# A single-core packed-attention and gated-convolution kernel: another issue order for the same instructions

## The chip, the cores and the metric

The kernel runs on one core of a Trainium2 chip. The metric is the device time of one execution in microseconds. Its engines, as the profile names them, are TensorE (PE, with PEld for the loads of its stationary operand), VectorE (DVE), ScalarE (ACT), GpSimd (POOL) and SyncE (SP), which issues all of the kernel's transfers (SPq). PSUM is the memory into which PE writes.

## The reference

Two attentions in a row, then a gated convolution with two matrix products. Batch 8, 8 heads, 576 positions, head size 64, 32 packed queries; the model width is 512.

```python
def sm_attn(qq, kk, vv):
    s = scale * np.matmul(qq, kk.transpose(0, 1, 3, 2))
    s = s - np.max(s, axis=-1, keepdims=True)
    a = np.exp(s)
    a = a / (np.sum(a, axis=-1, keepdims=True) + 1e-09)
    return np.matmul(a, vv)
p_packed = sm_attn(p, k, v)
out = sm_attn(q, p_packed, p_packed)
...
for k in range(K):
    gate_pre += conv_w[k][None, None, :] * xp[:, k:k + S, :]
gate = 1.0 / (1.0 + np.exp(-gate_pre))
val = x @ w_val
return (gate * val @ w_out).astype(np.float32)
```

`x` is the attention's output with the heads side by side, and `xp` is `x` with four rows of zeros ahead. The three weights come as double-precision numbers.

## The kernel before

Each of the eight batches goes through the same steps, and every kind of step is a Python generator (in the list `streams`) that issues a few instructions and then yields. Which generator goes on next is set by a long string, `ORDER`: a token such as `v0` takes the generator `v` of batch 0 one yield further, `v0.3` three yields, and a bar ends the stage in which the double-precision weights are turned into pairs of single-precision ones. The class `InOrder` makes each engine issue its instructions in exactly the order in which the tokens made them, SP's transfers too. So the string is the order, on all engines at once, and an instruction that waits holds up everything behind it on its engine.

The letters of the tokens, with the names that the instructions have in the profile:

- `K`, `V`, `Q`, `P`, `L`: transfers issued by SP. K and Q of a batch come in two halves (km, qm), V in two halves (vm) and a small rest (v), P for two batches at a time (p), the weights as blocks (cw_words, wv_words, wo_words).
- `C`: the convolution's weights; PE writes cwps. `W`: the value weights. `O`: the output weights, split into woh and wol by ACT, DVE and POOL.
- `k`, `q`: K and Q turned. In batches 0 and 1 PE turns them (kt, qt, and pTt for P), ACT copies them out; from batch 2 on DVE does it (kT, qT).
- `a`: the first attention, on the packed queries: scores s1 on PE, the row's maximum nb on DVE, the exponential on ACT, transposes at on PE, copies a1t on ACT, the product with V (pv) on PE.
- `p`: the packed result turned (ppTt on PE). `c`: the taps of the convolution multiplied in (ppk on POOL). `w`: the packed result times the value weights (wp on PE, wph and wpl).
- `s`, `t`: the second attention: scores s2 on PE, transposes t, maxima mx and sums sm on DVE, the subtraction and the scaling on POOL (DVE in batch 0), the exponential on ACT, and from them a, a2h and a2l.
- `g`: the gate, in two halves (gate on PE, sig on ACT). `v`: the value product, in two halves of two blocks (val on PE, then sig on DVE, gvh on ACT, gvl on DVE).
- `o`: the last product with woh and wol. Two batches together have nine chunks of 128 rows; o_2_1 is chunk 1 of batch 2's list. A chunk is 12 products on PE, a copy osb on ACT and two stores by SP. An even batch makes the chunks 0 to 3 of its pair, an odd one 4 to 8. The last batch makes its five chunks side by side, and only the last quarter of each chunk by itself.

In this text an index behind a name is the batch, and behind it the half or block: gate_2_1 is the second half of batch 2, val_0_1_0 the first block of the second half of batch 0.

What binds the order is the memory in which PE writes: one buffer `quad` for s1, s2 and gate, one buffer `big` for cwps, pv, wp and val, and two buffers `mid` for the transposes and the chunks of o. Each must have been read by ACT or DVE before the next one writes to it. Of K and Q there are five buffers together (`m`), of V two, of osb two, and of the weight blocks five.

The tokens run in two parts, before and behind the bar:

```python
before, after = ORDER.split("|")
with tc.tile_pool(name="stage", bufs=1) as stage:
    run(before)
late = ctx.enter_context(tc.tile_pool(name="late", bufs=1))
gvh = late.tile([P, NC, 2 * S], F32R, name="gvh")
gvl = late.tile([P, NC, 2 * S], F32R, name="gvl")
run(after)
```

gvh and gvl lie where the stage had its memory, so they wait for the last step on the weights. All instructions are recorded in the helper `InOrder`, so every row of the profile has its line, L61; the names tell the steps apart.

Of the kernel before, what the change touches and what calls it, by code (L numbers as in the profile page):

```python
# [26 lines left out]


ORDER = """
K0 P0 k0.6 K0 L0 C0.2 L0 k0 Q0 L0 Q0 k0.2 C0.4 k0.3 V0 k0.2 k1 k0 W0.2 a0 C0 V0 L0 q0.5 k1 a0.3 q0 k1 C0 q0 a0 q0 a0  # L30
q0.2 a0.4 C0 W0.5 V0 W0 a0.2 W0.6 L0 q0.2 W0 a0 L0 a0 p0 W0.2 p0.2 C0 W0.2 p0 O0.2 s0 W0.2 C0 W0 O0 K1 k1 K1 V1 W0
O0 s0 k1 s0 k1.2 Q1 k1.2 s0.2 k1.2 W0.2 s0 W0 O0.2 k1 O0 w0 k1 s0 Q1 t0 L0 V1 k1 c0 O0 w0 k1 s0 q1 s0 t0 a1 t0 q1.2
t0 q1 a1.3 V1 q1 t0 O0 q1 a1 c0 O0 q1.2 P2 t0.2 W0.2 w0 t0.2 a1.5 q1 O0.2 L0 O0 L0 K2.2 a1.2 t0 a1 O0 a1 O0 t0.2 q1
k2 O0 p1 O0 p1 k2 O0 g0 O0.3 p1 g0 O0.6 K3 q1 O0 k2 p1 q1 O0.3 k2 g0.2 O0.5 v0 O0.2 c1 v0 V2 O0 s1.2 O0 | v0 s1 v0.3
s1.2 a2 v0 s1 a2 v0 s1.2 V2 v0 k3 v0 V3 t1.2 v0 a2 s1 a2 o0 V2 v0 t1 o0 v0 a2 o0 v0 a2.2 t1.2 a2 t1 a2 v0 w1.2 t1 a2
o0 k3 t1 o0 a2.2 w1 Q2.2 K3 t1 c1 t1 a2 t1.2 g1 a2 v1 p2 k3.2 K4 P4 V4 p2 g1 p2 q2 k4 v1 p2 a3 o0 v0 Q3 K4 a3 V4
a3.3 q2 a3 v1.2 o0 v1 k4 a3 o0 s2.2 o0.2 s2.2 v1 s2 k4 a3 o0 s2 Q3 s2 v1.2 s2 a3 k5 k4 g1 v1 g1 t2 o0 t2 V3 a3 V3
a3.2 v1 a4 t2.2 s2 a4 t2 a4 c2 a4.2 k5 a3 o1 a3 K5 v1 q3 K5 o1.3 t2 o1.2 v1 t2 a4 t2.2 v1 t2 p3 v1 P6 a4 t2 a4.2 c2
a4 t2 p3 w2 V5 v1 w2 v1 g2 V4 w2 p3 Q4 o1 q3 g2 V5 k5.2 p3 Q5 a4.2 Q4 s3 o1 a4 s3.6 g2 a4 k6 s3 t3 v2 g2 v2 o1.2 s3
v2 p4 t3.2 Q5 t3 v2.2 K7 t3 v2 p4 o1 p4 o1 t3 v2 t3.2 a5.2 v2.2 o2 v2.2 a5 o2 q4 V6 v2.2 V6 p4 a5.3 o1 v2 o1 c3 a5  # L40
q4 t3.2 s4 c3 t3 s4.3 a5.2 s4 w3 t3 g3 o1 w3.2 a5 s4 g3 v3 s4 o2 t4 k6 v3 K6 v3.2 a5 t4.3 g3 v3.2 g3 q5 v3 c4 o2
v2.2 K6 v3.2 k6 a5 o2 q5 v3 Q6 k6 o3.3 V5 o2 v3.4 s4 a6.2 a5 a6 s4 K7 V7 a5 a6 V7 c4 t4.2 p5.2 o2 p5 a6 k7 a6 p5 o2
t4.2 w4 v3 s5 t4 s5 t4 s5 t4 s5 w4.2 s5 t4 k7 s5.2 o3 V6 k7.2 a6.2 o3.2 v3 g4.2 v4.2 a6 v4 a6 o2 s5 t5 v4 g4 v4 o2
s5 v4 a6 v4 a6.2 g4 t5.6 o2 t5 a6 a7 v4 c5.2 o3.2 v4 a7 p6 Q6 v4 t5 o2 o4.2 Q7 o4 v4.3 t5 a7 o3.4 a7.2 t5 p6 o4 t5
p6 v4 a7 w5 g5 q6 V7 p6 o4 w5.2 a7 v4.2 v5 q6 g5 v5 a7.2 v5 s6 v5 o4 v5 Q7 o4 v5.2 a7 o3 s6.2 o4 s6 q7 s6.2 t6 a7.3
g5 v5 a7 o3 s6 p7.2 s6 g5 t6 v5 o3 c6 v5.2 o4 t6.2 o5 v5 t6.2 c6 v5.2 o5 s6 q7 o5 v5 o5 p7.2 o5 t6 w6 t6 s7 t6.2
s7.2 o4 w6 t6.2 g6 s7 w6 v6 g6 s7.2 v5 o5 s7 t7 o4 g6 v6.3 s7 v6.2 t7 o5 g6 c7.2 t7 v6.3 s7 o5 o6 t7.3 v6.3 t7.2 o5
v6 o5 t7.2 v6 o4 t7.2 o5.2 w7 g7 o6 w7.2 g7 v7.4 g7 v7 o5 v7.3 o5 g7 v7 o6.2 v6 v7 o5 v6 v7 o6.2 v7.5 o7.28 o6 o7.2
o6.5
"""  # L50


# [701 lines left out]
```

## Time and profile before

| | |
|---|---|
| device time, three runs | 327.05, 328.51, 329.1 us; median 328.51 |
| the profiled execution | 327.33 us |
| its span, first to last instruction | 325.5 us |
| mean granted clock of PE | 0.952 |
| transfers | 43.62 MB, 33.57 read and 9.44 written |

The profile is one execution on the chip. PE's and PEld's instructions are counted apart; a wait is put down to what released it last, and "issue" stands where nothing in the profile released it. A row of the view by stretches of time gives, behind the two times and their length, the busy time of PE, PEld, DVE, ACT and POOL with the number of instructions behind x, then the granted clock of PE, the mean busy share of the 16 DMA engines and the GB/s. The rows of the chain and of the timeline begin with the start in us and the time taken.

### The profile page before, as it was taken

Reading aid. Unit: us, or ns where it says so; the run is one execution under the profiler, and the core shown is the slowest. Engines: PE = TensorE matmul, PEld = TensorE weight load, DVE = VectorE, ACT = ScalarE, POOL = GpSimd, SP = SyncE. Lnnn points to the kernel's source line nnn. Section 1 sums busy time; section 2 is a strip of 40 time slices with the busy share of each in tenths; the row PEclk is TensorE's granted clock in tenths of the full one; section 3 lists DMA queues with packets and bytes.
Section 4 is the critical chain, followed back from the end, with each engine's and each line's share of the span. In section 5 each row is a group of like instructions: output and inputs, shape, how many; then the busy total and the mean of one; then the engine's idle time right before and its main releaser. Section 6 shows DMA issues by size and latency. Waiting matters only on the chain.

```text
span 325.5 us, 9362 instructions
## 1 busy us (share of the span) xinstructions
PE 286.8 (88%) x4116; PEld 218.6 (67%) x4116; DVE 190.7 (59%) x304; ACT 150.2 (46%) x280; POOL 77.4 (24%) x84
## 2 busy tenths in 40 slices
PE   0978959779989689969999799999999999999964
PEld 0756536567767467758688567787778678688843
DVE  0157887869856754848778559345674756434010
ACT  2695777628533525253454545426345344524021
POOL 3016644843002320124032013040024250100000
PEclk9997878979979969999999899999999999999999
DMA  7999489904995905977352674145403203303055
GB/s 215 304 243 266 125 167 364 198 14 133 294 237 126 238 6 122 241 279 151 64 163 72 167 135 102 41 105 115 107 18 74 43 2 66 65 3 66 0 113 114
DMA packets 32731, 43.62 MB, mean 134 GB/s; under 512 B 10634, under 2 KB 18866, under 8 KB 32690
## 3 DMA queue, kind: packets, MB, share of 16 engines
q1 hardware_dynamic: 32690, 43.02, 54.0%
q8 instruction: 32, 0.52, 0.7%
q14 instruction: 9, 0.07, 0.1%
HBM read 33.57 MB, written 9.44 MB: 132 GB/s over the span
## 4 chain that ended last, share of the span: by engine, by line
PE 74%; DVE 8%; DMA 5%; ACT 4%; issue 3%; POOL 3%; SPq 1%; ACTq 0%; POOLq 0%; DVEq 0%
PE o L61 31%; PE val L61 15%; PE gate L61 10%; PE s L61 6%; PE wp L61 3%; PE kt L61 2%; PE pv L61 2%; PE at L61 2%; DMA vm<-in_v_dram 2%; DVE kT L61 1%; DMA v<-in_v_dram 1%; SPq L61 1%; DMA p<-in_p_dram 1%; DVE wo_top L61 1%; DVE wo_words L61 1%
## 5 line engine op out<-in xcount | busy, mean ns | idle before, releaser
L61 PE MATMUL o<-woh,gvh 128*128 128x512 f32 x144 | 60.1, 417 | 2.6 <-ACT osb L61 1.7
L61 PE MATMUL o<-wol,gvh 128*128 128x512 f32 x144 | 58.6, 407 | 0.0
L61 PE MATMUL o<-woh,gvl 128*128 128x512 f32 x144 | 58.0, 403 | 0.0
L61 PE MATMUL gate<-a,ppk 32*64 32x288 f32 x1280 | 44.0, 410 | 0.9 <-ACT sig L61 0.6
L61 PE MATMUL val<-a2h,wph 128*128 128x288 f32 x128 | 40.1, 314 | 5.1 <-issue 3.0
L61 ACT COPY osb<-o 128x512 f32<-128x512 f32 x34 | 19.8, 587 | 53.4 <-PE o L61 39.0
L61 DVE SCALAR_TENSOR_TENSOR sig<-sig,val 128x576 f32<-128x576 f32 x32 | 23.8, 744 | 31.2 <-PE val L61 28.9
L61 ACT CAST gvh<-sig 128x576 fp32r<-128x576 f32 x32 | 21.4, 673 | 39.5 <-DVE sig L61 36.1
L61 PEld LDWEIGHTS o<-woh,gvh 128*128 128x128 f32 x144 | 28.3, 197 | 15.2 <-issue 5.2
L61 PE MATMUL val<-a2h,wpl 128*128 128x288 f32 x128 | 38.3, 300 | 0.0
L61 PE MATMUL val<-a2l,wph 128*128 128x288 f32 x128 | 38.3, 299 | 0.0
L61 POOL TENSOR_TENSOR t<-t,mx 128x576 f32<-128x576 f32 x14 | 16.6, 1191 | 90.6 <-DVE mx L61 90.6
L61 PEld LDWEIGHTS gate<-a,ppk 32*64 32x64 f32 x1280 | 29.0, 133 | 13.4 <-issue 5.4
L61 POOL TENSOR_TENSOR t<-t,sm 128x576 f32<-128x576 f32 x14 | 17.1, 1219 | 72.4 <-DVE sm L61 58.8
L61 PEld LDWEIGHTS o<-woh,gvl 128*128 128x128 f32 x144 | 28.5, 198 | 6.5
L61 DVE TENSOR_TENSOR gvl<-sig,gvh 128x576 fp32r<-128x576 f32 x32 | 25.2, 790 | 12.0 <-ACT gvh L61 11.7
L61 PEld LDWEIGHTS o<-wol,gvh 128*128 128x128 f32 x144 | 28.5, 198 | 5.0
L61 PEld LDWEIGHTS val<-a2h,wph 128*128 128x128 f32 x128 | 24.5, 192 | 10.1 <-issue 4.0
L61 PEld LDWEIGHTS val<-a2h,wpl 128*128 128x128 f32 x128 | 24.6, 192 | 3.4 <-issue 2.9
L61 PEld LDWEIGHTS val<-a2l,wph 128*128 128x128 f32 x128 | 24.6, 192 | 0.0
L61 ACT ACTIVATE sig<-gate 128x1152 f32<-128x1152 f32 x16 | 18.1, 1132 | 13.7 <-PE gate L61 13.6
L61 DVE TENSOR_REDUCE nb<-s 128x1 f32<-128x576 f32 x16 | 12.0, 750 | 11.5 <-PE s L61 6.3
(96 smaller groups left out, 435.2 us busy)
## 6 DMA issues: line engine op xcount, KB each, us to landing
km<-in_k_dram SPq DMA_DIRECT2D x16, 576.0 KB, 7.7
qm<-in_q_dram SPq DMA_DIRECT2D x16, 576.0 KB, 6.7
out_dram<-osb SPq DMA_DIRECT2D x72, 128.0 KB, 2.4
vm<-in_v_dram SPq DMA_DIRECT2D x16, 512.0 KB, 10.6
wv_words<-in_moe_w_val_dram SPq DMA_DIRECT2D x4, 512.0 KB, 13.8
wo_words<-in_moe_w_out_dram SPq DMA_DIRECT2D x4, 512.0 KB, 9.8
p<-in_p_dram SPq DMA_DIRECT2D x16, 64.0 KB, 4.4
v<-in_v_dram SPq DMA_DIRECT2D x8, 128.0 KB, 6.3
```

The source lines that it names most:

```text
L61: made = getattr(self.engine, op)(*args, **kw)
```

## The change

Only the string `ORDER` is another. Every generator is the same, and so is every instruction that it issues; the string is one line shorter, so the helper's line is L60 in the listing of the changed kernel.

```diff
 ORDER = """
-K0 P0 k0.6 K0 L0 C0.2 L0 k0 Q0 L0 Q0 k0.2 C0.4 k0.3 V0 k0.2 k1 k0 W0.2 a0 C0 V0 L0 q0.5 k1 a0.3 q0 k1 C0 q0 a0 q0 a0
...
-v6 o5 t7.2 v6 o4 t7.2 o5.2 w7 g7 o6 w7.2 g7 v7.4 g7 v7 o5 v7.3 o5 g7 v7 o6.2 v6 v7 o5 v6 v7 o6.2 v7.5 o7.28 o6 o7.2
-o6.5
+P0 L0.2 C0 L0 k0 C0.2 k0 C0 K0 C0 W0 C0 k0 C0 K0 C0 W0 L0 C0 L0 C0 W0.6 k0 W0 k1 W0 Q0 k0.5 Q0 V0 k0.4 V0.2 W0.5 k0
...
+o6.2 v6 t7 o5.3 w7.3 o6.2 o5 g7.2 v7 g7 v7.5 v6 v7 g7 o6 v7.3 o7 v7 o6 v7 o6 o7 v7.3 o7.2 v7 o7.24 o6.2 o7 o6 o7
```

It moves steps everywhere. Three places follow. In these rows a name carries the number of its buffer, and a gate is named after its half alone.

SP's queue at the program's start, before:

```order
L61 DMA km_0_82<-in_k_dram 128x2x576
L61 DMA p_84<-in_p_dram 32x8x64 x4
L61 DMA km_1_110<-in_k_dram 128x2x576
L61 DMA cw_words<-in_moe_conv_w_dram 40x128
L61 DMA wv_words<-in_moe_w_val_dram 128x1024
L61 DMA qm_0_120<-in_q_dram 128x2x576
L61 DMA wv_words<-in_moe_w_val_dram 128x1024
L61 DMA qm_1_124<-in_q_dram 128x2x576
L61 DMA vm_148<-in_v_dram 64x8x256 x2
L61 DMA wv_words<-in_moe_w_val_dram 128x1024
L61 DMA v_0_268<-in_v_dram 64x8x64
L61 DMA wv_words<-in_moe_w_val_dram 128x1024
```

and now:

```order
L60 DMA p_82<-in_p_dram 32x8x64 x4
L60 DMA cw_words<-in_moe_conv_w_dram 40x128
L60 DMA wv_words<-in_moe_w_val_dram 128x1024 x2
L60 DMA km_0_107<-in_k_dram 128x2x576
L60 DMA km_1_115<-in_k_dram 128x2x576
L60 DMA wv_words<-in_moe_w_val_dram 128x1024 x2
L60 DMA qm_0_153<-in_q_dram 128x2x576
L60 DMA qm_1_167<-in_q_dram 128x2x576
L60 DMA vm_169<-in_v_dram 64x8x256 x2
L60 DMA v_0_185<-in_v_dram 64x8x64
```

P, the convolution's weights and two blocks of the value weights are now ahead of K; on PE cwps follows pTt at once and stands ahead of the kt transposes of batch 0.

SP's queue around the small load of V for batch 5 (v_5), before; osb_4 and osb_1 are the chunks o_3_4 and o_2_1:

```order
L61 DMA out_dram<-osb_8_2058 64x512 x2
L61 DMA out_dram<-osb_0_2016 64x512 x2
L61 DMA km_0_2207<-in_k_dram 128x2x576
L61 DMA km_1_2295<-in_k_dram 128x2x576
L61 DMA qm_0_2320<-in_q_dram 128x2x576
L61 DMA out_dram<-osb_4_2338 64x512 x2
L61 DMA v_5_2342<-in_v_dram 64x8x64
L61 DMA out_dram<-osb_1_2315 64x512 x2
L61 DMA km_1_2443<-in_k_dram 128x2x576
```

and now; osb_0 is the chunk o_2_0, vm_2249 and vm_2324 are V of the batches 7 and 6:

```order
L60 DMA km_0_1895<-in_k_dram 128x2x576
L60 DMA p_1902<-in_p_dram 32x8x64 x4
L60 DMA qm_1_2000<-in_q_dram 128x2x576
L60 DMA km_1_2008<-in_k_dram 128x2x576
L60 DMA out_dram<-osb_6_1968 64x512 x2
L60 DMA v_5_2057<-in_v_dram 64x8x64
L60 DMA qm_0_2096<-in_q_dram 128x2x576
L60 DMA out_dram<-osb_0_2113 64x512 x2
L60 DMA vm_2249<-in_v_dram 64x8x256 x2
L60 DMA km_0_2300<-in_k_dram 128x2x576
L60 DMA vm_2324<-in_v_dram 64x8x256
```

v_5 stood behind the stores of o_3_4 and now stands ahead of the stores of o_2_0. In the same way V of batch 3 moved: its second half (vm) and its rest (v_3) stood behind the stores of o_0_3; now the second half stands ahead of the stores of o_0_0, and the rest ahead of those of o_0_2.

PE around pv_5, before (s_6 is s1_6, o_2 is o_2_2):

```order
L61 MATMUL s_6_2363<-kT_1_2322,pT_1866 32x288 x2
L61 MATMUL s_6_2363<-kT_0_2311,pT_1866 32x288 x2
L61 MATMUL s_6_2363<-kT_1_2322,pT_1866 32x288 x2
L61 MATMUL pv_2400<-vm_1646,a1t_2062 32x64 x32
L61 MATMUL pv_2400<-v_5_2342,a1t_5_2063 32x64 x8
L61 MATMUL o_2_2459<-woh,gvh 128x512
L61 MATMUL o_2_2459<-wol,gvh 128x512
L61 MATMUL o_2_2459<-woh,gvl 128x512
```

and now (gate_0 is gate_3_0, wp is wp_3):

```order
L60 MATMUL at_9_2092<-ident,a_5_1954 64x128 x2
L60 MATMUL wp_2101<-wv,ppT_1607 32x512 x8
L60 MATMUL gate_0_2115<-a_1_76,ppk_1874 64x288 x40
L60 MATMUL pv_2164<-vm_1541,a1t_1993 32x64 x32
L60 MATMUL pv_2164<-v_5_2057,a1t_5_1994 32x64 x8
L60 MATMUL s_6_2211<-kT_0_2098,pT_2002 32x288 x2
L60 MATMUL s_6_2211<-kT_1_2158,pT_2002 32x288 x2
```

pv_5 stood between s1_6 and a chunk of o and now stands between gate_3_0 and s1_6. gate_4_1, pv_6 and s1_7 follow one another in the same way (before: pv_6, s1_7, with small transposes and a chunk ahead of them), and so do gate_5_0, pv_7 and gate_5_1. Of the rest of PE's order the prediction uses these: s2_2 now comes behind val_1_0_0 and s1_3 behind val_1_0_2, where before s1_3 came behind val_1_0_0 and s2_2 behind a chunk of o; o_0_3 moved from between s2_2 and gate_1_1 to behind val_2_0_0; and pv_4 with gate_2_1 stays as it was.

At the end: before, o_6_2 and o_6_3 came behind the chunks 4 to 8 of the last batch; now o_6_2 is done ahead of them, and o_6_3 comes just before the last stores of chunk 8.

More of the change, by code (lines that the diff above doesn't have):

```diff
@@ L29 @@
 ORDER = """
-K0 P0 k0.6 K0 L0 C0.2 L0 k0 Q0 L0 Q0 k0.2 C0.4 k0.3 V0 k0.2 k1 k0 W0.2 a0 C0 V0 L0 q0.5 k1 a0.3 q0 k1 C0 q0 a0 q0 a0
[L31 to L44, printed above, removed]
@@ L45 @@
-p6 v4 a7 w5 g5 q6 V7 p6 o4 w5.2 a7 v4.2 v5 q6 g5 v5 a7.2 v5 s6 v5 o4 v5 Q7 o4 v5.2 a7 o3 s6.2 o4 s6 q7 s6.2 t6 a7.3
-g5 v5 a7 o3 s6 p7.2 s6 g5 t6 v5 o3 c6 v5.2 o4 t6.2 o5 v5 t6.2 c6 v5.2 o5 s6 q7 o5 v5 o5 p7.2 o5 t6 w6 t6 s7 t6.2
-s7.2 o4 w6 t6.2 g6 s7 w6 v6 g6 s7.2 v5 o5 s7 t7 o4 g6 v6.3 s7 v6.2 t7 o5 g6 c7.2 t7 v6.3 s7 o5 o6 t7.3 v6.3 t7.2 o5
-v6 o5 t7.2 v6 o4 t7.2 o5.2 w7 g7 o6 w7.2 g7 v7.4 g7 v7 o5 v7.3 o5 g7 v7 o6.2 v6 v7 o5 v6 v7 o6.2 v7.5 o7.28 o6 o7.2
-o6.5
+P0 L0.2 C0 L0 k0 C0.2 k0 C0 K0 C0 W0 C0 k0 C0 K0 C0 W0 L0 C0 L0 C0 W0.6 k0 W0 k1 W0 Q0 k0.5 Q0 V0 k0.4 V0.2 W0.5 k0
@@ new lines @@
+W0 k0 W0 a0 W0 q0 W0.2 q0.3 L0 a0 W0 q0.3 a0 W0.2 a0 V1 q0.4 a0 q0 W0 C0 K1 W0 Q1 W0.2 a0.6 K1 a0.3 p0 k1 p0 O0 p0.2
+W0 s0 w0 O0 k1 O0.5 s0 O0 w0 s0 O0 s0 k1.3 L0 s0 V1 O0 s0.2 k1 t0 k1.2 s0 k1.3 O0 k1.3 t0 K2 O0 a1 s0 O0 c0 t0 O0 t0
+a1 Q1 c0 q1 O0 t0.2 O0 q1.2 a1.2 q1 t0 V1 t0 w0 O0 t0 a1.3 L0 O0 a1.2 q1 a1 q1.2 P2 O0 a1 O0.5 a1 O0 t0.3 k2 q1 a1
+g0 q1 L0 O0.4 a1 k2.2 p1.3 g0 O0 g0 K2 q1 k3 k2 p1 V2 O0.3 K3 O0 v0 O0.2 g0 O0 q1 v0 O0 q1 s1.3 O0 s1 O0 | v0.2 s1
+v0.3 V3 a2 V2 V3 a2 v0 s1 t1 v0 t1 v0 o0 Q2 a2.2 s1 v0 V2 v0 K3 s1 o0.2 t1 v0.2 a2.2 t1 a2.2 Q2 t1 s1 t1 a2 w1 k3 t1
@@ new lines @@
+a2 o0 a2 c1 K4 w1 t1 w1 a2 t1 k3 a2 P4 t1 Q3 a2 t1 q2 Q3 t1 c1 v0 g1 q2 p2 k3 o0 p2.2 g1 K5 p2 v1.3 v0 s2 K4 s2.2 v1
+o0 s2 V4 V3 v1 k4 v1 a3 k4 o0 a3.3 s2 a3 k4 o0 s2 a3 s2 a3 t2 a3 g1 q3 v1 a3.2 g1 k4 v1 o0 v1.2 a3 v1 a4 s2 a3 c2 k5
+q3 a3 V4.2 o1 a4.4 Q4 V5 v1 a3 t2.2 p3.2 v1 Q4 a4 c2 s2 t2.2 o1 v1 a4 k5 p3 V5 t2.2 o1 w2 a4 p3 k5 s3 K5 t2.2 s3 w2
+t2 s3.2 w2 s3 t2 o1 t2 a4 s3 t3 g2 Q5 s3 o1 v2 g2 t3 v2.3 q4.2 a4 o0 a4.2 o1 a4.2 s3 v1 o0 v1 g2 t3 k5 p4 s3 c3.2 g2
+v2.2 o0 K6 p4.2 P6 v2 a5 o1 a5 t3.3 a5.2 v2 a5 o1 t3 a5 k7 p4 v2 a5 Q5 k6.2 t3 v2 a5 K6 s4 v2 a5 t3 o1 s4 v2 s4 V5
@@ new lines @@
+v2 o2 t3.2 v2 t3 a5.3 Q6 k6 w3.2 o2 g3 o2 k6 w3 q5 a5 g3 a5 p5 a6.3 V7 a6 V7 v3.3 s4 o1 a6 v3.2 k7 K7 o2 o1 v3 s4.2
+t4 V6 q5 t4 o2 o1.2 p5 k7 p5 Q6 p5 v2 v3 o1.2 v2 v3 o2 s4.2 g3 t4.2 v3 s4 g3 a6 o3.2 o2 t4 o2 V6 v3 t4.4 v3.2 o3 q6
+v3 o3 t4.3 o2 o3.2 a6.2 v3 c4 s5 w4 s5 V6 c4 s5 Q7 a6 w4 K7 w4 g4 v4 g4 v4 o2 s5 v4 s5 a6 v4 s5 v4 v3 a6 v4 s5 g4 v4
+a6.2 t5 k7 a6 q7 g4 a7 p6.2 c5 a7 o2 t5.2 a7.3 v4 a7 p6 v4 q6 Q7 p6 o4 t5 s5.2 t5 a7 s6 a7 v4 o4 a7 t5.2 v3 o4 s6.3
+a7 o2 v4.2 o3 v4.2 o4 t5.2 o3 v4 c5 s6 a7 V7 s6 t5.3 a7 w5 o3 w5 g5.2 w5 o4 t6.4 s6.2 a7 s6 a7 g5 v5.2 q7 o3.3 v4 v5
@@ L50 @@
+t6 v5 c6 v5 t6 v5 o4 v5 o3 g5 v5.2 o5 v5.4 o5 o3 o5.2 t6.5 o5 v5 p7.2 o4 p7 o3 o4 t6 w6 c6 w6 g6 p7 w6 v6 g6 v6 o5
+s7 v6 s7 v5 s7.2 o4 v5 v6.3 s7.3 t7 s7 o5.2 v6 o4.2 t7 v6.2 t7.2 o5 o4 o5.2 g6.2 c7 s7 t7 v6 o6.2 v6.3 c7 v6 t7.6
+o6.2 v6 t7 o5.3 w7.3 o6.2 o5 g7.2 v7 g7 v7.5 v6 v7 g7 o6 v7.3 o7 v7 o6 v7 o6 o7 v7.3 o7.2 v7 o7.24 o6.2 o7 o6 o7
 """
```

## The prediction, made before the changed kernel ran

> **What bounds the kernel now.** I read the shares of the engines first, then the chain that ended last.
>
> ```profile
> span 325.5 us, 9362 instructions
> PE 286.8 (88%) x4116; PEld 218.6 (67%) x4116; DVE 190.7 (59%) x304; ACT 150.2 (46%) x280; POOL 77.4 (24%) x84
> q8 instruction: 32, 0.52, 0.7%
> PE 74%; DVE 8%; DMA 5%; ACT 4%; issue 3%; POOL 3%; SPq 1%; ACTq 0%; POOLq 0%; DVEq 0%
> ```
>
> TensorE (PE) is the bound: busy 88% of the span, and 74% of the chain. The change keeps every product, so what it can win or lose is PE's idle time (325.5 − 286.8 = 38.7 us) and the time in which PE ran at a low clock. Next I read what PE waited for. The columns are the total, the number of waits and the longest.
>
> ```profile
> PE s L61 <- issue: 3.3, 2, 1.7
> PE val L61 <- issue: 3.0, 1, 3.0
> PE pv L61 <- issue: 2.5, 1, 2.5
> PE pv L61 <- DMA v<-in_v_dram: 2.1, 2, 1.7
> PE val L61 <- DVE sig L61: 2.1, 1, 2.1
> PE pv L61 <- DVE nb L61: 1.4, 1, 1.4
> ```
>
> The odd group is "issue", 8.8 us: PE had nothing to wait for that the profile shows. To see what those four waits share I counted PE's instructions from the program's start to the moment of each (PE and PEld, the number behind x), and then looked at the stretch just ahead of the last three.
>
> ```profile
> 0.00:61.70 61.70, 44.51 (x726) 30.86 (x727) 36.76 (x63) 41.64 (x84) 27.40 (x39) 0.89 0.93 238
> 0.00:89.30 89.30, 68.23 (x1107) 49.70 (x1107) 59.07 (x101) 56.09 (x112) 37.28 (x48) 0.90 0.84 211
> 0.00:112.80 112.80, 88.67 (x1488) 64.70 (x1489) 74.55 (x126) 65.49 (x130) 42.03 (x52) 0.91 0.83 208
> 0.00:139.50 139.50, 112.26 (x1870) 82.58 (x1871) 90.57 (x151) 75.96 (x151) 46.30 (x56) 0.90 0.79 195
> 84.50:89.21 4.71, 4.71 (x106) 3.53 (x90) 4.66 (x7) 2.20 (x5) 0.00 (x0) 1.00 1.19 225
> 108.29:112.73 4.44, 3.05 (x144) 2.04 (x144) 3.11 (x6) 2.34 (x5) 1.97 (x2) 1.00 1.12 261
> 134.69:139.07 4.38, 4.14 (x164) 3.23 (x161) 3.15 (x6) 0.93 (x2) 2.12 (x2) 1.00 1.11 259
> 188.55:309.00 120.45, 120.32 (x1585) 93.66 (x1584) 63.72 (x96) 49.38 (x83) 21.43 (x19) 1.00 0.28 62
> ```
>
> The waits lie 381, 381 and 382 products apart, that is 762 to 764 instructions with the weight loads. The queue of instructions (q8) made 32 transfers, so one serves (4116 + 4116) / 32 = 257 instructions, and 762 is three of them. So I read the four waits as PE running dry at the end of a block of instructions whose successor had not landed. The last three rows but one say when: 196 to 325 instructions in under 5 us, with a DMA share (the column before the last) of 1.11 to 1.19, the queues full of loads. The last row is the counter-example: 120 us at a share of 0.28, in which PE is busy all but 0.13 us, though it holds dense neighbours too (pv_6 ahead of s1_7, pv_7 ahead of gate_5_1).
>
> The Trainium skill, "Runtime: NRT & Kernel Launch", section "Instruction fetch mechanics", says that instructions are refilled in 16 KiB blocks of 256 by the sequencer's own queue and that crossing a block is mostly hidden. The block agrees with the 257 above; "mostly hidden" does not, at waits of 1.7 to 3.0 us. By the rule alone these waits would have another cause; that is my second rival.
>
> Then the clock, the last column but two, and what runs at it:
>
> ```profile
> 92.98:96.39 3.41, 3.41 (x9) 2.63 (x8) 2.42 (x6) 2.22 (x5) 0.00 (x0) 0.50 1.07 161
> 113.46:120.28 6.82, 5.04 (x12) 3.80 (x12) 3.68 (x10) 1.23 (x3) 1.21 (x2) 0.50 0.05 16
> 120.28:142.00 21.72, 18.55 (x371) 14.09 (x370) 12.23 (x18) 10.45 (x19) 4.22 (x4) 1.00 0.81 201
> 185.14:188.55 3.41, 3.41 (x9) 2.67 (x10) 3.05 (x8) 1.63 (x5) 0.00 (x0) 0.50 0.90 240
> ```
>
> After the waits at 89.2, 112.7 and 182.9 us PE got half its clock, for one or two steps of 3.41 us; after the one at 139.1 it did not. A busy step at half clock does half its work, so it costs 1.71 us.
>
> **The change part by part.** The sum goes against the profiled execution, 327.33 us; its span is 325.5, and the median of the runs, 328.51, is 1.18 above it.
>
> ```profile
> 89.21 1.70 issue
> 92.27 4.54 PE o L61 x12
> 112.73 2.51 issue
> 176.03 2.75 PE o L61 x12
> 180.62 3.99 DMA v<-in_v_dram
> 185.07 4.54 PE o L61 x12
> 105.12 0.67 SPq L61 DMA_DIRECT2D vm<-in_v_dram  x1
> DMA to landing us min/median/max: 6.1/6.1/6.1
> ```
>
> (1) *The wait in s1_3.* 1.70, and the step at half clock behind it 1.71 (o_0_2 takes 4.54 where o_3_4 takes 2.75): 3.41.
>
> (2) *The wait around pv_3.* The page names DVE nb for the first 1.39 us, but pv_3 doesn't read nb; the second half of V of batch 3 was issued at 105.12 and landed 6.1 us later, at 111.2, and pv_3 began at 111.3. So it is a late load. Then 2.51 of issue, and 5.04 us of work at half clock, half of it lost: 2.52. Together 6.42. The change issues both halves of vm of batch 3 among the loads of batch 2, far ahead, and o_0_3 moves back, so that by a count of the order the block that ended inside pv_3 now ends behind o_1_4.
>
> (3) *The wait in front of val_2_0_0.* 3.00, with no low clock. pv_4 and gate_2_1 stay neighbours, but what filled the queues there (both halves of vm of batch 5, two loads of Q) is now issued about 15 us of PE's work earlier; near them one load of K and P of batch 6 are left. I take the whole 3.00 as gone; that it isn't is a part of rival C.
>
> (4) *The wait of pv_5.* v_5 was issued at 180.62, because its place in SP's queue is behind the stores of o_3_4, which wait for a copy of ACT. PE waited 1.71 and then had a step at half clock, 1.71: 3.42. Now v_5 stands ahead of the stores of chunk 0 of batch 2, and no store of batch 3 is ahead of it; by the order its load comes 13 us of PE's work before pv_5, and a load needed 3.99.
>
> Together 3.41 + 6.42 + 3.00 + 3.42 = 16.25 us. What the new order puts back:
>
> (5) *One wait of the kind may stay.* pv_2, gate_1_0, ppTt_2, val_1_0_0 and s2_2 follow one another as densely as the run ahead of s1_3 did, only with s2_2 in s1_3's place, and three of the loads that follow pv_2 are still issued there. Bounds: nothing (no load waiting at that moment, as in the row 188.55:309.00) and 3.41 (as before). I take 1.70 and an even chance of the low clock, 2.55, since the neighbouring row is that very place.
>
> (6) *Closer neighbours.* pv_5 and s1_6 now follow gate_3_0 at once, pv_6 stands between gate_4_1 and s1_7, pv_7 between gate_5_0 and gate_5_1.
>
> ```profile
> L61 ACT ACTIVATE sig<-gate 128x1152 f32<-128x1152 f32 x16 | 18.1, 1132 | 13.7 <-PE gate L61 13.6
> 111.28 1.45 PE pv L61 x79
> ```
>
> The PSUM tile of a gate is read by one ACT step of 1.13 us, and the next user of that tile has only pv, 1.45 us, as cover. A late ACT (one other step ahead of sig, 0.6 us) leaves 0.3 uncovered. Bounds: nothing, and 1.13 a place; I take 0.2 at three places, 0.6, nearer to the end at which ACT is free, since ACT is busy 46%.
>
> (7) *The end.* Before, the chunks 4 to 8 of the last product were followed by o_6_2 and o_6_3, 24 products; now by o_6_3 alone, and o_7_8's copy is the very last step.
>
> ```profile
> 310.10 0.50 PE L61 MATMUL o<-woh,gvh 128*128 128x512 f32 x1 [0.68 <-ACT osb L61]
> 313.92 0.50 PE L61 MATMUL o<-woh,gvh 128*128 128x512 f32 x1 [1.05 <-ACT osb L61]
> 321.10 0.59 ACT L61 COPY osb<-o 128x512 f32<-128x512 f32 x1 [1.69 <-PE o L61]
> ```
>
> The waits of 0.68 and 1.05 between those chunks stay. Two copies instead of one follow the last product: one more of 0.59, and its store's issue. Bounds: nothing (the first copy is done meanwhile) and 1.3; I take 0.7.
>
> (8) *The start*, up to o_0_0. The loads of P, of the convolution's weights and of two blocks of value weights now stand ahead of K, and cwps ahead of the kt transposes.
>
> ```profile
> 0.00:8.00 8.00, 0.00 (x0) 0.00 (x0) 0.00 (x0) 1.68 (x2) 3.02 (x14) 1.00 0.79 215
> 9.46 1.72 PE kt L61 x8
> 26.40 2.85 PE cwps L61 x20
> 65.75 1.30 POOL wol L61
> 69.26 3.25 PE val L61 x12
> ```
>
> kt waits for some 1.3 MB more than before; at 215 GB/s I put it at 12.6 us, 3.1 later (an estimate). cwps leaves its place at 26.40, where it took 2.85, and moves into time that PE idled anyway. That leaves +0.3. The part ends at val_0_1_0, which stood 2.10 us for the chain POOL wol, ACT gvh, DVE gvl, DVE sig. A start later by 3.1 with only these 2.10 as cover gives +1.0; the 2.10 gone and the small P load first (0.4) gives −2.5. The nearest row is that chain, whose steps the change doesn't shorten: I take 0.
>
> (9) *GpSimd beside other VectorE steps.* VectorE's steps may get shorter or longer; from 73 us on the list of PE's waits has no VectorE row that isn't explained above. PE's own work covers it: 0. If that cover is gone at one place, the price is that of one GpSimd step and one VectorE step, about 2 us.
>
> Sum: −16.25 + 2.55 + 0.6 + 0.7 + 0 = −12.4, so 314.9 for an execution like the profiled one. The median lies 1.18 above that execution; I add half of it: 315.5 us.
>
> **The rivals.**
>
> *A: the low clock comes as often.* The steps at half clock after o_0_0 cost 1.71 + 2.52 + 1.71 = 5.94. For it: the wait of 3.00 brought no low clock and that of 1.70 did, so length alone does not set it. Against: each of the three follows a wait. Time: 315.5 + 5.9 = 321.4. The Trainium skill, "TensorE: Matmul & The Clock Gate", section "What's actually happening", gives windows of 3413 ns that run freely and a drop after at least one idle window. The steps of 3.41 us agree; that a whole window must be idle does not, with waits of 1.70 and 2.51 us ahead of two of the drops.
>
> *B: the waits stay.* If "issue" isn't the block of instructions, or a new block ends as badly, the waits of 1.70, 2.51 and 3.00 come back, with 4.23 of low clock: 11.44, of which 2.55 are in the sum already. Time: 315.5 + 8.9 = 324.4. For it: a block ends every 257 instructions whatever the order.
>
> *C: slower.* gate, pv and a score run one behind another at 70 or more instructions per us, as dense as the row at 134.69: pv_4 with gate_2_1, and the three places of (6). If loads fill the queues at these four, each costs 3.00 and a step at half clock, 4.71. It decides when all four do: 315.5 + 18.8 = 334.3; three give 329.6, no change. Against: the last three lie where before the DMA share was 0.28.
>
> *D: the start keeps its delay.* kt is 3.1 later, and nothing makes it up: 318.6.
>
> **How the numbers follow.** The forecast 0.46 (its own range 310 to 319), D 0.08, A 0.20, B 0.16, C 0.10. A measurement of this kernel tells about 1% from no change, so faster means under 325.2 and slower over 331.8. Faster: 0.46 + 0.08 + 0.19 of A + 0.05 of B = 0.78. Same: 0.01 of A, 0.09 of B, 0.03 of C = 0.13. Slower: 0.07 of C, and 0.02 of B where it comes with D = 0.09. Low end of the range: without (5) and with the start at −2.5 it is 310.5; 1 us less for a shorter end gives 309.5. High end: B, 324.5. Outside lie C, some of B and a little of the forecast, about 0.2.
>
> **What would show it.** Right: PE's waits show "issue" below 3 us after 75 us, no wait of pv for V, one step at half clock or none between 75 and 309 us, and PE's last product by 310 us. (5) is seen at s2_2. (8) is right if o_0_0 starts at 72 ± 2 us. A shows as half clock without waits; B as issue waits at other places, still some multiple of 257 instructions apart; C as issue in or behind s1_6, s1_7 and gate_5_1. Wrong would be a new wait of PE for ACT or DVE over 2 us.

## The result and the profile after

| | before | changed |
|---|---|---|
| device time, median of four runs | 327.98 us (327.05 to 329.1) | 316.99 us (313.66 to 318.51) |
| the profiled execution, its span | 327.33, 325.5 us | 313.66, 311.9 us |
| PE busy | 286.8 us, 88% | 281.6 us, 90% |

The ratio is 0.963, 95% interval 0.9535 to 0.9724: 3.7% faster. The medians in this text are over all executions, while a ratio leaves out those more than 1.5% above the fastest of the same kernel (here the one of 318.51), so the medians alone, 11.0 us apart, give a little less. The profiled execution of the changed kernel is the fastest of its four, so its profile is a little better than the median; a second profile of the same kernel, below, belongs to an execution of 317.95 us.

What PE waited for in the changed kernel, first in the whole span and then between 75 and 295 us (total, number, longest):

```profile
PE pTt L60 <- ACT cw_top L60: 6.5, 1, 6.5
PE pv L60 <- ACT a1t L60: 2.5, 1, 2.5
PE s L60 <- ACT kT L60: 2.0, 2, 1.7
PE s L60 <- issue: 1.6, 1, 1.6
PE o L60 <- ACT osb L60: 1.5, 2, 0.8
PE o L60 <- issue: 1.3, 1, 1.3
PE o L60 <- DVE osb L60: 0.8, 1, 0.8
```

```profile
PE gate L60 <- ACT a L60: 0.4, 1, 0.4
PE wp L60 <- DVE sig L60: 0.4, 1, 0.4
```

Between 75 and 295 us no wait for issue is left and none for V; two waits of 0.4 us are all. The next view, by stretches (busy time of PE, PEld, DVE, ACT, POOL, then clock, DMA share, GB/s), has the same part of before in its first row:

```profile
75.00:309.00 234.00, 223.28 (x3227) 173.19 (x3226) 143.21 (x225) 100.36 (x182) 42.89 (x39) 0.97 0.46 113
```

```profile
75.00:300.57 225.57, 222.26 (x3247) 171.82 (x3246) 143.44 (x222) 102.78 (x185) 43.65 (x40) 1.00 0.46 113
300.57:303.99 3.42, 3.42 (x10) 2.68 (x9) 0.69 (x1) 0.00 (x0) 0.00 (x0) 0.50 0.58 124
82.37:88.26 5.89, 5.89 (x172) 5.07 (x172) 5.89 (x9) 3.80 (x8) 0.00 (x0) 1.00 0.79 191
124.68:128.72 4.04, 4.04 (x162) 2.91 (x161) 4.04 (x6) 2.30 (x5) 0.00 (x0) 1.00 0.37 74
144.97:150.58 5.61, 5.61 (x233) 3.77 (x225) 3.19 (x5) 2.93 (x4) 0.00 (x0) 1.00 0.40 83
```

Before, PE idled 10.7 us of that part and ran at a mean clock of 0.97; now it idles 3.3 us, 2.4 of them at the end, at a clock of 1.00. About as many products (3247 against 3227) take 8.4 us less. The last three rows are dense stretches, up to 458 instructions in 5.6 us, and not one made PE wait: the DMA share is 0.37 to 0.79 there, where in the three stretches of the prediction it was 1.11 to 1.19. The row at 300.57 is new: a step at half clock at the very end.

### The profile page after: what moved, and what is told of

It reads as the page before. It is cut to its first block, busy times and chain, and to the rows that moved or that the text cites. A ratio compares the mean times of both kernels' runs of the same rounds, so it can differ in the third digit from the quotient of the medians.

```text
span 311.9 us, 9379 instructions
## 1 busy us (share of the span) xinstructions
PE 281.6 (90%) x4116; PEld 214.3 (69%) x4116; DVE 189.4 (61%) x304; ACT 150.0 (48%) x280; POOL 79.5 (25%) x84
## 4 chain that ended last, share of the span: by engine, by line
PE 76%; ACT 7%; DVE 6%; DMA 5%; issue 2%; POOL 0%; ACTq 0%; SPq 0%; POOLq 0%
PE o L60 30%; PE val L60 15%; PE gate L60 13%; PE s L60 6%; DMA wo_words<-in_moe_w_out_dram 4%; PE wp L60 3%; PE pv L60 3%; PE at L60 2%; PE kt L60 2%; PE cwps L60 1%; ACT kT L60 1%; ACT a L60 1%; DVE sig L60 1%; ACT qT L60 1%; DVE qT L60 1%
## 5 line engine op out<-in xcount | busy, mean ns | idle before, releaser
L60 PE MATMUL o<-woh,gvh 128*128 128x512 f32 x144 | 58.0, 403 | 2.4 <-ACT osb L60 1.5
L60 PE MATMUL o<-wol,gvh 128*128 128x512 f32 x144 | 57.1, 396 | 1.3 <-issue 1.3
L60 PE MATMUL o<-woh,gvl 128*128 128x512 f32 x144 | 57.0, 396 | 0.0
L60 PE MATMUL gate<-a,ppk 32*64 32x288 f32 x1280 | 44.5, 415 | 0.8 <-ACT a L60 0.4
L60 DVE SCALAR_TENSOR_TENSOR sig<-sig,val 128x576 f32<-128x576 f32 x32 | 23.9, 748 | 30.1 <-PE val L60 25.1
L60 PE MATMUL val<-a2h,wph 128*128 128x288 f32 x128 | 39.7, 310 | 0.2 <-DVE sig L60 0.2
L60 ACT COPY osb<-o 128x512 f32<-128x512 f32 x34 | 19.7, 585 | 39.5 <-PE o L60 33.3
L60 PEld LDWEIGHTS gate<-a,ppk 32*64 32x64 f32 x1280 | 29.6, 135 | 13.2 <-issue 4.8
L60 POOL TENSOR_TENSOR t<-t,mx 128x576 f32<-128x576 f32 x14 | 19.2, 1369 | 73.5 <-DVE mx L60 73.5
L60 PE MATMUL val<-a2h,wpl 128*128 128x288 f32 x128 | 37.7, 294 | 0.0
L60 PE MATMUL val<-a2l,wph 128*128 128x288 f32 x128 | 37.7, 294 | 0.0
L60 ACT CAST gvh<-sig 128x576 fp32r<-128x576 f32 x32 | 21.4, 673 | 33.1 <-DVE sig L60 30.5
L60 PEld LDWEIGHTS o<-woh,gvh 128*128 128x128 f32 x144 | 27.5, 191 | 11.4 <-ACT osb L60 2.4
L60 POOL TENSOR_TENSOR t<-t,sm 128x576 f32<-128x576 f32 x14 | 16.9, 1207 | 64.5 <-DVE sm L60 60.4
L60 PEld LDWEIGHTS o<-wol,gvh 128*128 128x128 f32 x144 | 27.5, 191 | 6.4 <-issue 1.7
L60 PEld LDWEIGHTS o<-woh,gvl 128*128 128x128 f32 x144 | 27.3, 190 | 6.1
L60 DVE TENSOR_TENSOR gvl<-sig,gvh 128x576 fp32r<-128x576 f32 x32 | 24.8, 782 | 10.5 <-ACT gvh L60 10.1
L60 PEld LDWEIGHTS val<-a2h,wph 128*128 128x128 f32 x128 | 24.0, 188 | 7.1 <-issue 2.3
L60 ACT ACTIVATE sig<-gate 128x1152 f32<-128x1152 f32 x16 | 18.1, 1133 | 15.9 <-PE gate L60 15.9
L60 PEld LDWEIGHTS val<-a2h,wpl 128*128 128x128 f32 x128 | 24.1, 188 | 0.6
L60 PEld LDWEIGHTS val<-a2l,wph 128*128 128x128 f32 x128 | 24.0, 188 | 0.0
L60 POOL TENSOR_TENSOR ppk<-ppd,cwb 128x320 f32<-128x320 f32 x16 | 13.8, 874 | 16.2 <-PE gate L60 16.1
```

Source lines behind the costliest of these rows:

```text
L60: made = getattr(self.engine, op)(*args, **kw)
```

## The experiments

Twelve runs, one of them the changed kernel again. Each time is a median beside runs of the kernel before on the same chip; a ratio is to those.

**1. Only the loads of V moved.** Before, with these tokens moved in the string, nothing else:

```diff
-v0 V3 t1.2
+v0 V3.2 t1.2
...
-K4 a3 V4 a3.3
+K4 a3 V4 V3 a3.3
...
-t2 V3 a3 V3 a3.2
+t2 a3.3
...
-k6 v3 K6
+k6 v3 V5 K6
...
-k6 o3.3 V5 o2
+k6 o3.3 o2
```

> The kernel before, with two loads of V moved forward in SP's queue: the second half and the rest of V of batch 3 no longer stand behind the stores of o_0_3, and v_5 no longer behind those of o_3_4. If the issue waits are blocks of instructions that land late, pv_5's wait (1.71) and the half-clock step behind it (1.71) go, but at pv_3 the 1.39 us that pv_3 starts earlier are only added to the issue wait, because the block lands when it did before: some 3.4 us less in all, issue waits of 2.5 us or more stay in or behind pv_3, and those in s1_3 and ahead of val_2_0_0 stay as they were. If the 1.39 is a cost of its own (the sum of the prediction adds it), 4.8 us less. If V was not what pv_3 waited for, its first wait stays at 1.4.

322.83 us, ratio 0.9932 (0.9882 to 0.9981): 2.2 us less, with much uncertainty (0.6 to 3.9; the expected 3.4 lies in it, 4.8 does not). PE around pv_3 in its profile:

```profile
112.19 1.10 PE L60 MATMUL pv<-vm,a1t 128*32 128x64 f32 x64
113.22 0.42 PE L60 MATMUL pv<-v,a1t 64*32 64x64 f32 x15
114.61 0.21 PE L60 MATMUL pv<-v,a1t 64*32 64x64 f32 x1 [0.97 <-issue]
```

pv_3 begins without a wait, so V was what it waited for, and pv_5's wait is gone too. The issue wait inside pv_3 is 0.97 and not 2.51. The expectation that it would stay was wrong: the block's own transfer, in the instruction queue, began at 112.31 us, 1.33 ahead of the wait, where before it began at 112.80, with the wait. So the late load of V probably was itself one of the transfers that the block of instructions came behind; no run shows that apart. Waits of 2.0 in s1_3 and 3.3 ahead of val_2_0_0 stay, as expected, and a new one of 1.0 is in a gate.

**2. Blocks moved, order kept.** Before, with 48 small products at PE's start (each is two instructions on PE and two loads of weights, 192 in all):

```diff
+    fill = one("fill")
+    for n in range(48):
+        pe.matmul(fill[:NP, :NP], ident[:NP, :NP], ident[:NP, :NP], start=True, stop=True)
     before, after = ORDER.split("|")
```

> The kernel before in its own order, with 48 small products more on TensorE at the very start, where it idles for 8.4 us: 192 instructions, so every block of 256 ends 192 instructions earlier in the program. Nothing else is changed. If the issue waits are ends of blocks, those in pv_3 (2.51) and ahead of val_2_0_0 (3.00) go, since by count no block ends in a dense stretch there any more; the one of s1_3 moves to the end of s1_3 or behind it and is at most as long; the time falls by 5 to 9 us with the half-clock steps behind them. If the waits belong to the steps themselves, all of them stay where they were and the time is that of before within 1%.

318.05 us, ratio 0.9741 (0.9604 to 0.9877). More work, the same order, and some 8 us less. PE's waits between 75 and 300 us:

```profile
PE s L61 <- issue: 1.9, 1, 1.9
PE pv L61 <- DVE a L61: 1.0, 1, 1.0
PE pv L61 <- DMA v<-in_v_dram: 0.9, 1, 0.9
```

The issue waits of pv_3 and val_2_0_0 are gone. That of s1_3 moves on within the step; here is PE behind it, before and now:

```profile
90.90 1.37 PE L61 MATMUL s<-kT,pT 32*32 32x288 f32 x36 [1.70 <-issue]
```

```profile
93.03 0.67 PE L61 MATMUL s<-kT,pT 32*32 32x288 f32 x4 [1.92 <-issue]
```

Four of PE's instructions are left of s1_3 where 36 were: with the loads of weights the wait is 64 instructions further on, and 64 is 256 less 192. This is the decisive run: the waits belong to the place where a block of instructions ends, not to the step in which they are seen.

The traces say so in two more ways. The view by stretches leaves out the few instructions of PE's own sequencer. With them, the four waits of before begin behind instruction 1473, 2241, 3009 and 3777, exactly three times 256 apart, and each of the 29 waits for issue of 0.5 us or more in the fourteen profiles begins 193 or 194 instructions behind a multiple of 256. And each of these waits ends 1.3 to 1.7 us after a transfer of the instruction queue has landed.

**3 to 5. More transfers at one place.** The changed kernel with four copies of 576 KB within the chip's memory, issued by SP at three places:

```diff
+    extra = nc.dram_tensor("extra", [4, P, 2 * NE * D], F32, kind="Internal").ap()
...
+        for n in range(4):
+            sp.dma_start(
+                extra[n].rearrange("a (h x) -> a h x", h=2), rows[:, 2 * (n % 2) : 2 * (n % 2) + 2]
+            )
+            yield
```

Behind the stores of o_2_0:

> The changed kernel with four copies of 576 KB from K's memory to unused memory, issued by SP right behind the stores of o_2_0, which is when the block is asked for that ends inside s1_6 (rival C's place: gate_3_0, pv_5, s1_6). If a block waits behind other transfers, its transfer starts 3 to 6 us after it would otherwise, and an issue wait of 1.5 to 4 us stands in or right behind s1_6 or pv_5, perhaps with a step at half clock behind. If blocks don't suffer from transfers, no wait is there and the profile around 145 to 155 us is that of the changed kernel.

Behind the stores of o_1_7:

> The control of the run before: the same four copies, issued behind the stores of o_1_7, some 11 us later, where blocks last 12 us and more. Both if the block theory holds and if not: no issue wait between 140 and 180 us. If the copies themselves slow TensorE (by the memory or the queues, not by the blocks), a wait appears here as well.

Ahead of the stores of o_2_0:

> As the run with four copies behind the stores of o_2_0, where the copies began at 150.6 us, after the block inside s1_6 had landed, and so tested nothing; now the copies stand ahead of those stores and start some 4 us before that block is asked for. If a block waits behind other transfers: PE waits for issue 1.5 to 4 us in pv_5, s1_6 or just behind, where the changed kernel has none, perhaps with a step at half clock behind. If not: no wait there.

Single executions: 317.13, 315.17 and 317.87 us, all within the changed kernel's own spread, so only the traces count. The first began its copies at 150.6 us, when the block had landed, and tested nothing. The control shows no issue wait between 140 and 180 us. The third started them at 143.1; here are the stretch from gate_3_0 to s1_6 and PE's rows at its end:

```profile
148.15:154.30 6.15, 4.67 (x171) 3.01 (x164) 3.19 (x5) 2.93 (x4) 0.00 (x0) 1.00 0.96 326
```

```profile
152.15 0.67 PE L60 MATMUL s<-kT,pT 32*32 32x288 f32 x3
154.32 1.57 PE L60 MATMUL s<-kT,pT 32*32 32x288 f32 x61 [1.50 <-issue]
```

With a DMA share of 0.96 where the changed kernel has 0.40, a wait of 1.50 us stands inside s1_6, three products in. The block's own transfer began at 152.06 us, 0.76 ahead of the wait; in the changed kernel the same block began to come 2.8 us before PE needed it. So transfers ahead of a block make PE wait, at the low end of what was expected and without a low clock. It is one execution at one place.

**6 and 7. One half of the order each.** The string up to the bar from one kernel, then the other's tokens in their order, without those already used. The line with the bar, in the changed kernel and in the first of the two:

```diff
-g0 q1 L0 O0.4 a1 k2.2 p1.3 g0 O0 g0 K2 q1 k3 k2 p1 V2 O0.3 K3 O0 v0 O0.2 g0 O0 q1 v0 O0 q1 s1.3 O0 s1 O0 | v0.2 s1
+O0 p1 k2 O0 g0 O0.3 p1 g0 O0.6 K3 q1 O0 k2 p1 q1 O0.3 k2 g0.2 O0.5 v0 O0.2 c1 v0 V2 O0 s1.2 O0 | k3 s1.2 v0.2 s1 v0.3
```

> The order of before up to the bar, then that of the changed kernel for all steps that are left. By the prediction the start is worth nothing and the rest everything: within 2 us of the changed kernel, 315 to 319, no issue wait after 75 us. If the start carries part of the gain, 319 to 325.

> The other half: the order of the changed kernel up to the bar, then that of before. By the prediction as slow as before within 2 us, 324 to 330, with issue waits again inside s1_3, in pv_3 and ahead of val_2_0_0, and a late v_5. If the start carries part of the gain, the time is 3 us or more below before, with those waits still there.

With the old start and the new rest: 314.37 us, ratio 0.956 (0.9499 to 0.9621). With the new start and the old rest: 332.64 over all ten executions, ratio 1.0103 (1.0037 to 1.0169), by which it is slower than before by 3.4 us (1.2 to 5.5). So the rest holds the whole gain, and the new start costs something rather than nothing. In the second of them the issue waits are back, behind the same instructions 2241, 3009 and 3777 (the last now falls in a gate); its PE waits between 75 and 310 us begin with:

```profile
PE gate L60 <- issue: 3.3, 1, 3.3
PE pv L60 <- issue: 2.5, 1, 2.5
PE pv L60 <- DMA v<-in_v_dram: 1.8, 1, 1.8
PE s L60 <- issue: 1.6, 2, 1.4
```

**8. Blocks moved in the changed kernel.** The 48 products of experiment 2, in the changed kernel:

> The changed kernel with the same 48 small products at the start, so that all blocks end 192 instructions earlier. If the changed order is good because of where its blocks end, this moves them: by count one is now asked for at the moment at which the loads behind pv_2 are issued and ends in s2_2 or val_1_0_2, and issue waits of 1 to 3 us come back there, one or two in all after 75 us, and the time is 1 to 6 us above the changed kernel. If the changed order is good whatever the blocks do, the time stays within 1 us of it, or gains the 1 us by which PE is warm at the start.

323.43 us, ratio 0.9818 (0.9746 to 0.989): of the 3.7% about half is lost, some 6 us. Its largest waits in the whole span:

```profile
PE gate L60 <- issue: 4.8, 2, 3.1
PE val L60 <- issue: 2.7, 1, 2.7
```

Waits came back, but not where the expectation had put them: 3.1 is in gate_0_1 at 61.8 us, 2.7 in val_0_0_2, and a third, of 1.6, in gate_2_0. The five microseconds or less ahead of each, and ahead of s2_2:

```profile
57.30:61.84 4.54, 4.16 (x88) 2.55 (x72) 1.44 (x2) 2.85 (x6) 1.97 (x2) 0.95 1.12 201
67.50:72.17 4.67, 4.67 (x95) 3.20 (x82) 1.26 (x2) 2.54 (x4) 1.40 (x2) 0.95 1.14 179
123.20:127.70 4.50, 4.50 (x57) 3.09 (x55) 4.36 (x7) 1.81 (x4) 1.16 (x1) 1.00 1.12 225
92.70:97.70 5.00, 5.00 (x137) 4.14 (x130) 5.00 (x7) 2.25 (x6) 0.00 (x0) 1.00 0.80 234
```

A block does end in s2_2, as counted, but it had landed 3.3 us before PE came to it. So the theory is confirmed; the count gives the place of a block's end, and not whether PE waits there. The three rows with a wait have a DMA share of 1.12 to 1.14, and at 112 to 177 instructions they are less dense than the row without one (267 instructions, share 0.80). So density is not needed. The share alone does not decide either: before, a block ended at 135.1 us behind 5 us at a share of 1.14, and PE did not wait, because that block had landed at 132.5.

**9. The changed kernel once more.**

> The changed kernel once more, on the same chip and beside the same runs of before as the two that follow: 314 to 319, ratio to before 0.955 to 0.972. Its start should again vary from run to run: o_0_0 between 70.7 and 75 us.

316.13 us (312.63 to 319.65, six runs), ratio 0.9648 (0.9576 to 0.972). PE in s2_1, first in this profile, then in the first one of the same kernel:

```profile
62.97 1.28 PE L60 MATMUL s<-qT,ppT 64*32 64x256 f32 x36
67.61 0.64 PE L60 MATMUL s<-qT,ppT 128*32 128x32 f32 x28 [3.36 <-ACT gvh L60]
```

```profile
62.16 1.28 PE L60 MATMUL s<-qT,ppT 64*32 64x256 f32 x36
65.06 0.45 PE L60 MATMUL s<-qT,ppT 128*32 128x32 f32 x28 [1.62 <-issue]
```

The same wait at the same product, 3.36 and 1.62 us long. s2_1 does not read gvh, so the name is only that of the last release; by its place, behind instruction 1474, and because it ends 1.6 us after an instruction block has landed, it is the block's end that before showed as 1.65 of issue. It is one thing that differs between executions of this start.

**10. The weights' buffers.** The changed kernel with one figure changed:

```diff
-    "words": 5,
+    "words": 6,
```

> The changed kernel with six buffers for the weight blocks, so that the second block of the output weights (wo1) is asked for at once and not only when a buffer comes free at 37.4 us. In the changed kernel it lands at 49.9 us, ACT's step on it stands ahead of copies that PE needs, and PE waits 2.0 us in s1_1 and 2.5 in pv_1. If that load is what makes the new start late, those two waits go, o_0_0 starts 2 to 4 us earlier than in the other runs with this start (73 to 75.2) and the time falls to 312 to 314. If not, the start stays where it is, within 1 us, or moves later because the early load takes the queues from K and Q.

313.97 us, ratio 0.956 (0.9505 to 0.9616). pv_1's wait for a1t is gone, and s1_1 has no wait of 2 us in it, and o_0_0 starts at 72.36 us: 0.7 to 2.9 earlier than in the other profiles with this start, apart from the first one (70.70) and the one with moved blocks (80.88). PE comes to the block's end in s2_1 at 62.1 us, where the second profile of the changed kernel has 64.3, but waits 3.4 us there. So that load does make PE wait and is a part of what makes the start late, in one profile; how early the start ends is also set by that block. Whether the time is better than that of the changed kernel (0.9576 to 0.972) isn't settled: the intervals overlap.

**11 and 12. Another end, and both together.** The old start, the new rest, and an end in which the last quarter of all five chunks of the last batch comes first and their copies after it, into buffers that are free by then; then the same with six buffers for the weight blocks:

```diff
+        for c in accs:
+            product(accs[c], c, NC - 1)
+            yield
         for c in chunks:
             ops = accs.get(c)
             if ops is None:
                 ops = one(f"o_{b}_{c}")
-                for n4 in range(NC - 1):
+                for n4 in range(NC):
                     product(ops, c, n4)
-            product(ops, c, NC - 1)
-            yield
-            osb = tile_of("osb", [P, DM], F32, f"osb_{b}_{c}")
+                yield
+            tag = "osb" if b < B - 1 else "t2" if c % 2 else "sig"
+            osb = tile_of(tag, [P, DM], F32, f"osb_{b}_{c}")
```

> The order of before up to the bar and the changed order behind it, and another end: the last quarter of all five chunks of the last batch comes first, and then their copies, into buffers that are free by then (t2 and sig), with o_6_3 on PE meanwhile. If the end's cost lies in PE's waits for copies between the chunks (2.3 us in all) and the half-clock step that may follow, those are gone and the time is 2 to 4 us under that of the run with the same start without this end, 310.5 to 312.5. If SP's twelve stores at the end bind instead, no gain.

> The run above with six buffers for the weight blocks instead of five, so that the second block of the output weights no longer waits for a buffer. If that wait holds the start back, val_0_1_0's wait of 3.1 us shrinks and the time falls by 1 to 3 us more. If DVE's and POOL's own steps on the weights bind, nothing changes, or the earlier load delays V of batch 1 and costs up to 2 us.

312.67 us, ratio 0.9583 (0.9532 to 0.9635), and 310.94 us, ratio 0.9516 (0.9456 to 0.9577); one of the six executions of the last took 490.78 us at a mean clock of 0.796, the other five 309.44 to 312.03. Without that one, the last version beats both kernels: its slowest, 312.03, lies under the fastest execution of the changed kernel beside it, 312.63. SP's queue at the end, in the run with the same start without the new end, and with it:

```profile
303.51 5.47 SPq L60 DMA_DIRECT2D out_dram<-osb  x6
```

```profile
301.10 7.51 SPq L60 DMA_DIRECT2D out_dram<-osb  x12
```

PE's waits between the chunks are gone, and PE's last product ends at 303.9 us where it ended at 305.9. But all twelve stores now come at once and SP needs 7.5 us for them, so most of it is given back: the spans are 311.4 and 311.7, and the ratios of the two versions (0.956 without the new end) don't differ. What the sixth buffer does is not shown: the two ratios overlap, o_0_0 starts at 72.91 and 72.52 us, and val_0_1_0's wait of 3.1 is down to 0.2 already without that buffer, where PE waits 2.5 us in s2_1, ahead of it. An issue wait of 1.4 in o_0_0, which only the profile with five buffers has, is more than half of the difference of their spans, 2.3.

## Why the prediction was right, step by step

The time, 316.99, is 1.5 us above the forecast, inside its range. For the profiled execution the sum said 314.9, and it took 313.66.

- **(1) to (4), the 16.25 us.** All the waits of these steps are gone from the profile, and so are the half-clock steps behind three of them. That the three issue waits among them are ends of blocks is shown by moving the blocks alone, both ways (experiments 2 and 8), and by the count; that transfers make them long, by one run (experiment 5). The reading of 762 as three times 257 was rough, 10 short: three blocks are 768, and the view leaves out PE's sequencer. That V was a cost of its own at pv_3 is shown by experiment 1; the step counted its wait and the issue wait as two things, while moving V shortened both.
- **(5), one wait that stays: 2.55 taken, 0 measured.** The stretch up to s2_2 is as dense as thought (344 instructions in 5.89 us), but the DMA share in it is 0.79, not 1.19. A block does end in s2_2, but its transfer began 4.0 us before PE needed it, where in s1_3 before it began 1.2 us ahead of the wait. The step leaned on the place and not on the transfers that are under way when the block is asked for.
- **(6), closer neighbours: 0.6 taken.** No wait at any of the three places.
- **(7), the end: 0.7 taken, about 2.8 measured.** From PE's last product to the end it takes 5.8 us where it took 4.5, 1.3 more, as the bound had it; and a step at half clock follows the three waits for copies, 1.71 more, that before did not have. The three waits are 0.2 shorter. The step had no low clock in it.
- **(8), the start: 0 taken.** Mis-sized. kt began at 12.41 us, close to the 12.6 of the step, though that figure does not follow from its terms (1.3 MB at 215 GB/s are 6.0 us, not 3.1). In the profiled execution o_0_0 started at 70.70 us, 1.6 earlier than before. But in five other profiles with the new start (three with the copies, the second profile, the new start with the old rest) it came at 73.05 to 75.24, with six buffers at 72.36, and with moved blocks at 80.88; in the six with the old start (one of them with moved blocks, one with six buffers) it came at 72.31 to 74.34. The median of the five is 75.2, of the six 72.6. A start later by about 2.5 is the more usual case, more than the bound of +1.0; the chain over wol, which was to set its end, makes val_0_1_0 wait only 0.2, and the block's end in s2_1, a wait of 2.4 to 4.2 in these five, takes its place.
- **(9)** PE waits for VectorE once after 75 us, for 0.4: the cover holds.

So for the profiled execution: −16.25 + 2.8 − 1.6, and 1.29 for a new issue wait in o_0_0, gives −13.8; measured −13.67. In the second profiled execution, 317.95, the start is 2.9 later instead, o_0_0 has no issue wait, and the end has two steps at half clock (3.1 lost) and waits 0.4 shorter: −16.25 + 2.9 + 1.3 + 3.1 − 0.4 gives −9.35; measured −9.38. The right total came in part from errors that cancel: (5) too dear, (7) and (8) too cheap.

Of the rivals, A is half seen: the low clock went with the waits, yet it came back at the end where waits of the same length had not brought it before. B fell with experiment 2. C did not come: the dense rows at two of its places have a DMA share of 0.37 and 0.40. Its mechanism is real, as experiment 5 shows, at 1.50 us. D is right about the start as a rule, and not in the first profile; experiment 7 puts it at 1.2 to 5.5 us.

The Trainium skill, "Runtime: NRT & Kernel Launch", section "Instruction fetch mechanics", calls the crossing of a block mostly hidden. Between 75 and 295 us of the changed kernel the trace agrees: 25 blocks end there, with no issue wait. At the 29 waits of experiment 2 it does not: they last 0.8 to 4.2 us.

What stays open: why the block's wait in the new start (s2_1, 1.62 to 4.17 us) varies so much between executions, and whether the low clock at the end depends on anything but the moment.

## What to carry to other kernels

In these traces a wait for "issue" that returns after a fixed number of PE's instructions was the end of an instruction block: count the instructions to it, the sequencer's too, before looking for a cause in the step itself, and test it by adding a few instructions at the start. PE waited where a block ended and the next had not landed, mostly while large loads filled the queues. Moving the blocks' ends removed two such waits, moving one load shortened one from 2.51 to 0.97 us, and putting loads in made one of 1.50. Such a gain hangs on where blocks end, so any later edit that adds or removes instructions can lose it: 192 small instructions cost this kernel some 6 us, and won 8 in the other order.

## What was not expected of the hardware

The same change of 192 instructions made one order 2.6% faster and the other some 2% slower. And executions of the changed kernel differ by 7 us (312.63 to 319.65 in ten). Of the 4.3 us between the two that were profiled, 3.0 are there when the transposes of batch 2's first attention begin (at_2_0, 76.59 and 79.55 us), and the rest comes at the end, where the second has two steps at half clock and the first has one.
